# Attention, routed experts and dense experts in one kernel: the place of the norms, of the query tail, of the loads and of the first expert's number

## The chip, the cores and the metric

The kernel runs on one core of a Trainium2 chip. The metric is the device time of one execution in microseconds; before the change the median of three runs is 2073.45 us.

## The reference

Three parts follow each other, all in float32.

1. Attention over 4 batches of 8 heads, 576 tokens, head size 64: causal softmax attention, and a memory part `phi(q) @ M_prev / (phi(q) . z_prev + 1e-6)` with `phi(x) = max(x, 0) + min(exp(x), 1)`. The two are mixed by `g = sigmoid(beta)` of each head.
2. The 2304 rows of 512 go through a routed layer: `logits = x @ w_gate + modality_bias`, each row goes to the one of 8 experts with the highest logit, `relu(x @ w1) @ w2` with 1024 hidden columns, times the softmax weight of that expert.
3. A dense layer: all 8 experts see all rows, and their outputs are summed with weights from 8 rounds of row and column normalisation.

## The kernel before, in words

**Attention** (lines 27 to 490) works in 16 units `u`; one unit is two heads of one batch. Its instructions stand in an order written out by hand (`tc.manual_schedule()`), and each engine runs its own in that order. A unit is pipelined over two turns of the loop `for u in range(1, NU)`: in turn `u` the scores, maxima and exponentials of unit `u` are made, while unit `e = u - 1` is transposed, multiplied with its values and written, and keys and queries of `u + 1` are transposed.

The steps that matter here: `high(u)` and `low(u)` (scores of the four full query tiles, L226, and their masks, L333 and L342), `last_scores(u)` (the last 64 queries of both heads, L235), `top(u, i)` (row maxima on VectorE, L243 and L245), `exps(u, i)` (ScalarE, L257 and L259), `ptrans(e, k)` (TensorE transposes the probabilities, VectorE or ScalarE copies them out, L281, L289, L295, L296, L300), `tails` (the 64-row tails of keys, queries and phi(q), copies L210, L213, L214, L215), `memory(e, part)` (L309) and `av(e, part)` (L321, output L323). `phi_a` multiplies phi(q) by `z_prev` (VectorE L133, GpSimd L134), `phi_b` makes the norms from the sums of that product (VectorE L148 to L151) and scales the tail (GpSimd L153), `phi_c` brings in the softmax sums and scales the rest. `gate_v` (L141) scales the values, `relu` (L121) and `phi_e` (L126) prepare phi. `bank()` hands out four PSUM banks in turn (`ps_t`, 4 buffers), so a step may wait for the last reader of the bank four allocations back.

Part 0 of `memory` and `av` covers queries 0 to 255, part 1 the others (`SPAN`). `busy(n)` issues `n` matmuls of zeros, whose result nobody reads.

**Loads.** `load(u, names, eng)` issues three transfers for each of k, q and v: one for each head and one for the 64-row tails of both. `prepare()` issues unit 0's on the sync engine's queue (SP) and unit 1's on ScalarE's.

**Router.** `batch(g)` takes a group of 128-token tiles (`GROUPS`) once their attention is done: logits, softmax weight, one-hot of the expert, row numbers; each scaled tile is then scattered to its expert's region (GpSimd, L504). It is a generator, and the loop's `some()` runs one step. The last group runs behind the attention. `table()` then works out from the counts which tiles of which expert follow each other, and `rt.busy(64)` stands behind it.

**Routed experts** (`routed_experts`): `e0 = reg(0, 0, 0, ...)` reads the first expert's number from the table on SP, then SP issues two pieces of its `w1` (L856), the first tile's rows (L864, behind all scatters), and the other weights. TensorE transposes the rows (L878) and starts with L907. **Dense experts** follow.

Of the kernel before, what the change touches and what calls it, by code (L numbers as in the profile page):

```python
# [12 lines left out]
I32 = mybir.dt.int32  # L13
# [13 lines left out]
def attention(ctx, tc, q, k, v, M_prev, z_prev, beta, xT, ident, router):  # L27
# [10 lines left out]
    ps_t = es.enter_context(tc.tile_pool(name="ps_t", bufs=4, space=PSUM))  # L38


    qTp, Mb, Rs, vt = [], [], [], []
    nrm = [c1.tile([128, NT, 2], F32, name=f"nrm{i}") for i in range(2)]
    zeros = c1.tile([128, 512], BF16, name="zeros")
# [12 lines left out]
    def prepare():  # L56

        nc.vector.memset(zeros, 0.0)
        busy(12)
        gb = c1.tile([128, H], F32, name="gb")  # L60
        nc.scalar.dma_start(gb, beta[None, :].to_broadcast([128, H]))
        nc.gpsimd.memset(mk, 0.0)
        nc.gpsimd.affine_select(out=mk, in_=mk, compare_op=ALU.is_ge, fill=-1e9, base=0,
                                pattern=[[-1, 128]], channel_multiplier=1)
        for i in range(2):
            t = c1.tile([128, 640], F32, name=f"qTp{i}")
            nc.gpsimd.memset(t[:, 512:], 0.0)
            qTp.append(t)
        load(0, "kq")
        load(1, "kq", nc.scalar)  # L70
        nc.vector.tensor_copy(idb, ident)
        nc.vector.tensor_copy(mk2[0:64], mk[0:64, 0:64])
        nc.vector.tensor_copy(mk2[64:128], mk[64:128, 64:128])
        nc.scalar.activation(gt, gb, AF.Exp, scale=-1.0)
        nc.vector.tensor_scalar(gt, gt, 1.0, None, ALU.add)
        nc.vector.reciprocal(gt, gt)
        nc.vector.tensor_scalar(om, gt, -1.0, 1.0, ALU.mult, ALU.add)
        for i in range(2):
            t = c1.tile([128, NP, 128], F32, name=f"Mb{i}")
            nc.gpsimd.memset(t, 0.0)  # L80
            Mb.append(t)
        for i in range(3):
            t = c1.tile([128, NT, 128], F32, name=f"vt{i}")
            nc.gpsimd.memset(t[0:64, 4], 0.0)
            vt.append(t)
        for i in range(2):
            t = c1.tile([128, S], F32, name=f"R{i}")
            nc.gpsimd.memset(t[:, 512:], 1.0)
            Rs.append(t)
# [90 lines left out]
    def keys(u):  # L180

        p = bank("tp")
        turn(p, ld[u, "k"])
        un[u] = {"kT": tr.tile([128, S], F32, tag="kT", name="kT"), "P": {}}
        nc.vector.tensor_copy(un[u]["kT"][:, :512], p)
# [16 lines left out]
    def tails(u, un1):  # L202


        p = bank("tl")
        if u is not None:
            nc.tensor.transpose(p[:, 0:128], ld[u, "q"][:, 4], ident)
        if un1 is not None:
            nc.tensor.transpose(p[:, 128:256], ph[un1][1][:, 4], ident)
            nc.vector.tensor_copy(un[un1]["pT"][:, 512:], p[:, 192:256])  # L210
        if u is not None:
            qt = qTp[u % 2]
            nc.vector.tensor_copy(un[u]["kT"][:, 512:], p[:, 0:64])  # L213
            nc.scalar.activation(qt[0:64, 512:576], p[0:64, 64:128], AF.Copy, scale=0.125)  # L214
            nc.vector.tensor_scalar(qt[64:128, 576:640], p[64:128, 64:128], 0.125, None, ALU.mult)  # L215

    sc = {}

# [80 lines left out]
            nc.tensor.transpose(p[:, 0:128], PM[:, 448:576], ident)  # L299
            nc.vector.tensor_copy(un[u]["pt4"], p[:, 0:128].rearrange("p (h q) -> p h q", h=2))  # L300

    SPAN = ((0, 256), (256, S))

    def memory(u, part):

        b, a = divmod(u, NP)
        q0, q1 = SPAN[part]
        un[u]["x", part] = x = bank("x")
        nc.tensor.matmul(x[:, :q1 - q0], Mb[b % 2][:, a], un[u]["pT"][:, q0:q1], start=True, stop=False)  # L309

    def av(u, part):

        b, a = divmod(u, NP)
        pt, vn, x = un[u]["pt"], vt[u % 3], un[u]["x", part]
        q0, q1 = SPAN[part]
        nj = (2, 5)[part]
        for j in range(nj):
            for h in range(2):
                qs = max(q0, j * 128)
                rhs = pt[:, h, j, qs:q1] if j < 4 else un[u]["pt4"][:, h]  # L320
                nc.tensor.matmul(x[h * 64:(h + 1) * 64, qs - q0:q1 - q0], vn[:, j, h * 64:(h + 1) * 64], rhs,  # L321
                                 start=False, stop=(j == nj - 1))
        nc.vector.tensor_tensor(xT[:, a, b * S + q0:b * S + q1], x[:, :q1 - q0], Rs[u % 2][:, q0:q1], ALU.mult)  # L323
# [18 lines left out]
            nc.tensor.matmul(s[:, h, 128:384].rearrange("p (i k) -> p i k", i=2), idb,  # L342
                             mk[:, None, :].to_broadcast([128, 2, 128]), start=False, stop=True)

    NU = B * NP
    with tc.manual_schedule():
        prepare()
        keys(0)
        queries(0)
        tails(0, None)  # L350
        load_b(0)
        load(0, "v")
        rt = router()
        rt.ps, rt.busy = ps_t, busy
        relu(0)
        rt.constants()
        phi_e(0)
        load(1, "v")
        load(2, "kq")
        high(0)  # L360
        for i in (3, 2):
            top(0, i)
            exps(0, i)
        keys(1)
        queries(1)
        tails(1, None)
        busy(8)
        low(0)
        for i in (1, 0):
            top(0, i)  # L370
        phi_a(0)
        relu(1)
        gate_v(0)
        for i in (1, 0):
            exps(0, i)
        busy(3)
        last_scores(0)
        busy(8)
        phi_e(1)
        top(0, 4)  # L380
        phi_b(0)
        phi_c(0)
        phi_a(1)
        back = rt.biases()

        def some():
            next(back, None)

        def finish(u):
            exps(u, 4)  # L390
            norm(u)

        for u in range(1, NU):
            e, nx = u - 1, u + 1 < NU
            if nx:
                load(u + 1, "v")
            if u + 2 < NU:
                if (u + 2) % NP == 0:
                    load_b((u + 2) // NP)
                load(u + 2, "kq")  # L400
            if u < 3:
                rt.clear(u - 1)
            finish(e)
            gate_v(u)
            if nx:
                relu(u + 1)
            high(u)
            top(u, 3)
            some()
            ptrans(e, 5)  # L410
            ptrans(e, 4)
            exps(u, 3)
            ptrans(e, 0)
            top(u, 2)
            exps(u, 2)
            ptrans(e, 1)
            if nx:
                keys(u + 1)
                queries(u + 1)
            inverse(e)  # L420
            low(u)
            ptrans(e, 2)
            phis(e)
            top(u, 1)
            top(u, 0)
            ptrans(e, 3)
            some()
            phi_b(u)
            ptrans(e, 6)
            ptrans(e, 7)  # L430
            exps(u, 1)
            exps(u, 0)
            tails(u + 1 if nx else None, e)
            last_scores(u)
            if nx:
                phi_e(u + 1)
            top(u, 4)
            phi_c(u)
            some()
            if nx:  # L440
                phi_a(u + 1)
            else:
                finish(u)
            memory(e, 0)
            memory(e, 1)
            av(e, 0)
            av(e, 1)
            if u % NP == 0:
                for _ in back:
                    pass  # L450
                back = rt.batch(u // NP - 1, ps_t)
            del un[e]

        e = NU - 1
        for _ in back:
            pass
        ptrans(e, 0)
        ptrans(e, 1)
        inverse(e)
        ptrans(e, 2)  # L460
        phis(e)
        ptrans(e, 3)
        memory(e, 0)
        av(e, 0)
        ptrans(e, 5)
        ptrans(e, 4)
        back = rt.batch(3, ps_t)
        next(back)
        ptrans(e, 6)
        ptrans(e, 7)  # L470
        next(back)
        tails(None, e)
        memory(e, 1)
        next(back)
        av(e, 1)
        for _ in back:
            pass
        for _ in rt.batch(4, ps_t, True):
            pass
# [3 lines left out]
NE = 8  # L483
# [8 lines left out]
HT = 384  # L492
NG = N // (2 * HT)
GTL = 2 * HT // 128
GROUPS = [range(0, 4), range(4, 9), range(9, 13), range(13, 15), range(15, 18)]
WHY = "the table is worked out on the chip and stays within its bounds"
ET = mybir.EngineType

# [27 lines left out]
class Router:  # L526
# [21 lines left out]
    def constants(self):  # L548
# [21 lines left out]
        self.pos = c.tile([128, NTILE], I32, name="pos")  # L570
        self.tab = [c.tile([128, 4], I32, name=f"tab{i}") for i in range(2)]
        self.num = c.tile([1, 2], I32, name="num")

        self.table_parts()

# [133 lines left out]
    def table(self, ps):  # L709
# [15 lines left out]
                                th[:, None, :].to_broadcast([128, NE, M1]), ALU.is_gt)  # L725
        nc.vector.tensor_copy(cnt, tp)
        nc.vector.tensor_reduce(nt[:, :NE], gm, AX.X, ALU.add)
        left, big = t1([NE], "left"), t1([NE], "bigr")
        nc.vector.scalar_tensor_tensor(left, nt[:, :NE], -float(TB), cnt, ALU.mult, ALU.add)
        nc.vector.tensor_scalar(big, left, float(HB), None, ALU.is_gt)  # L730
# [63 lines left out]
def tile_attention_moe_moe(ctx, tc, q, k, v, M_prev, z_prev, beta, modality_id, w_gate1, modality_bias, w1a, w2a,  # L794
# [10 lines left out]
    with ExitStack() as actx:  # L805
# [2 lines left out]
        rt = attention(actx, tc, q, k, v, M_prev, z_prev, beta, xT, ident,  # L808
                       lambda: Router(actx, tc, c, xT, ident, modality_id, w_gate1, modality_bias))
        rt.table(rt.ps)  # L810
        rt.busy(64)

    big = ctx.enter_context(tc.tile_pool(name="big", bufs=1))
    X = big.tile([128, KD, XW], F32, name="X")
# [16 lines left out]
def routed_experts(ctx, tc, rt, ident, X, raw1, raw2, split, w1, w2, early):  # L831
# [184 lines left out]
            else:  # L1016
                nc.scalar.copy(yl, p.rearrange("p (h t) -> p h t", h=2))

    e0 = reg(0, 0, 0, (ET.SP,), NE - 1)
    for j in range(2):  # L1020
        load1(e0, j)
    xr, loads = load_x(0, 0)
# [425 lines left out]
```

## Time and profile before

| | |
|---|---|
| median of 3 runs | 2073.45 us (2072.9 to 2074.33) |
| the profiled execution | 2072.47 us |
| its span, first to last instruction | 2070.7 us |
| TensorE busy | 2017.4 us (97%) |
| VectorE, ScalarE, GpSimd busy | 1471.6, 850.8, 783.9 us |

Attention takes the first 275 us, the routed experts run to about 545 us, the dense ones to the end. An engine that is busy is not yet the one that bounds a stage; what shows that is which waits end last there. Each wait in the trace names the engine, its line, and the instruction that released it.

### The profile page before, as it was taken

What the parts mean: (1) busy time and instruction counts of PE and PEld (TensorE: products, weight loads), DVE (VectorE), ACT (ScalarE), POOL (GpSimd) and SP (SyncE); (2) the same over time, 40 slices, a digit from 0 to 9 for tenths busy, and PEclk for the clock granted to TensorE, in tenths of its full rate; (3) what the DMA queues carried; (4) which work ended last, traced back from release to release, by engine and by line L of the source; (5) the groups of instructions that cost most, each with busy time, mean ns of one, the idle gap of its engine ahead of it and who ended that gap; (6) DMA issues with size and microseconds to landing.
All of it is one profiled execution on the core that took longest, in us unless ns stands there. A gap on an engine that the chain in (4) does not pass through costs nothing.

```text
span 2070.7 us, 31467 instructions
## 1 busy us (share of the span) xinstructions
PE 2017.4 (97%) x11499; PEld 1773.3 (86%) x11499; DVE 1471.6 (71%) x2551; ACT 850.8 (41%) x1793; POOL 783.9 (38%) x761
## 2 busy tenths in 40 slices
PE   8998999998899999999999999999999999999998
PEld 5666669998699889988889988998898988998887
DVE  6877767665687776667796667777688676677775
ACT  4566545554634333333343333333343433333332
POOL 6666510000133344344464334334356333333332
PEclk9999999999999999999999999999999999999999
DMA  6333166556512233444432222222223122222221
GB/s 157 91 81 85 44 207 226 184 194 208 162 51 62 72 71 62 62 68 76 62 110 64 62 78 66 62 77 67 62 72 102 62 71 72 62 68 76 62 63 40
DMA packets 236157, 187.36 MB, mean 90 GB/s; under 512 B 69028, under 2 KB 191956, under 8 KB 235988
## 3 DMA queue, kind: packets, MB, share of 16 engines
q1 hardware_dynamic: 228772, 175.08, 30.6%
q0 software_dynamic: 3616, 9.49, 1.3%
q8 instruction: 95, 1.56, 0.3%
q10 hardware_dynamic: 3600, 0.63, 0.2%
q14 instruction: 74, 0.61, 0.1%
HBM read 171.51 MB, written 13.64 MB: 89 GB/s over the span
## 4 chain that ended last, share of the span: by engine, by line
issue 31%; PE 24%; POOL 17%; DMA 0%; DVE 0%; ACT 0%; POOLq 0%; SPq 0%; DVEq 0%
PE y L1250 13%; PE prod L1179 11%; POOL T L1071 8%; POOL w1l L1065 7%; POOL out_dram L504 1%; DMA r<-in_moe_w_dram 0%; PE lq L1291 0%; POOLq L1071 0%; POOL S L1149 0%; POOL S L1150 0%; POOL S L1151 0%; DVE w2l L1065 0%; POOL S4l L1065 0%; POOL S L1148 0%; PE lg L1303 0%
## 5 line engine op out<-in xcount | busy, mean ns | idle before, releaser
L1065 POOL TENSOR_TENSOR w1l<-T,w1h 128x1024 fp32r<-128x1024 f32 x94 | 226.7, 2411 | 842.5 <-ACT w1h L1065 842.5
L1197 ACT ACTIVATE hh<-c 128x384 fp32r<-128x384 f32 x384 | 202.1, 526 | 829.5 <-DVE c L1193 828.6
L1250 PE MATMUL y<-w2h,hh 128*128 128x512 f32 x1152 | 453.3, 394 | 0.0
L1250 PE MATMUL y<-w2l,hh 128*128 128x512 f32 x1152 | 453.3, 393 | 0.0
L1250 PE MATMUL y<-w2h,hl 128*128 128x512 f32 x1152 | 452.6, 393 | 0.0
L1202 DVE SCALAR_TENSOR_TENSOR hl<-c,hh 128x384 fp32r<-128x384 f32 x384 | 418.1, 1106 | 1.1 <-ACT hh L1197 0.8
L1193 DVE TENSOR_TENSOR c<-prod,u 128x384 f32<-128x384 f32 x288 | 160.0, 556 | 156.0 <-PE prod L1179 153.0
L1250 PEld LDWEIGHTS y<-w2h,hh 128*128 128x128 f32 x1152 | 216.2, 188 | 32.8
L1250 PEld LDWEIGHTS y<-w2h,hl 128*128 128x128 f32 x1152 | 216.3, 188 | 28.5
L1250 PEld LDWEIGHTS y<-w2l,hh 128*128 128x128 f32 x1152 | 216.4, 188 | 27.9
L1071 POOL TENSOR_TENSOR T<-r 128x256 f32<-128x256 f32 x188 | 161.6, 859 | 7.1
L1071 POOL TENSOR_TENSOR T<-r,T 128x256 f32<-128x256 f32 x188 | 158.7, 844 | 14.0 <-issue 6.9
L1193 DVE TENSOR_TENSOR u<-prod,u 128x384 f32<-128x384 f32 x192 | 105.7, 551 | 58.1 <-PE prod L1179 57.8
L1193 DVE TENSOR_TENSOR u<-prod,p 128x384 f32<-128x384 f32 x96 | 53.4, 557 | 129.6 <-PE prod L1179 128.3
L1065 DVE TENSOR_TENSOR w2l<-r,w2h 128x512 fp32r<-128x512 f32 x188 | 136.9, 728 | 0.6 <-ACT w2h L1065 0.6
L1065 ACT CAST w2h<-r 128x512 fp32r<-128x512 f32 x188 | 106.7, 609 | 0.0
L1193 DVE TENSOR_TENSOR c<-prod,p 128x384 f32<-128x384 f32 x96 | 53.5, 557 | 70.8 <-PE prod L1179 65.0
L1065 DVE TENSOR_TENSOR w1l<-r,w1h 128x512 fp32r<-128x512 f32 (+1 forms) x188 | 103.7, 551 | 0.0
L1065 ACT CAST w1h<-T 128x1024 fp32r<-128x1024 f32 x94 | 97.0, 1032 | 1.0 <-POOL T L1071 1.0
L1207 ACT COPY p<-prod 128x384 f32<-128x384 f32 x96 | 46.2, 481 | 123.4 <-PE prod L1179 122.1
L1261 DVE SCALAR_TENSOR_TENSOR acc<-y,P,acc 128x512 f32<-128x512 f32 x126 | 92.4, 743 | 4.3 <-PE y L1250 4.3
L1065 ACT CAST w1h<-r 128x512 fp32r<-128x512 f32 (+1 forms) x188 | 94.5, 503 | 0.0
(388 smaller groups left out, 4167.7 us busy)
## 6 DMA issues: line engine op xcount, KB each, us to landing
r<-in_moe_w_dram SPq DMA_DIRECT2D x188, 512.0 KB, 4.3
r<-in_moe_w_dram SPq DMA_DIRECT2D x188, 256.0 KB, 3.1
xr<-xs_sorted SPq DMA_DIRECT2D x22, 256.0 KB, 5.0
vt<-in_v_dram SPq DMA_DIRECT2D x32, 128.0 KB, 2.6
xs_sorted<-zrow SPq DMA_DIRECT2D x16, 256.0 KB, 3.1
kn<-in_k_dram SPq DMA_DIRECT2D x30, 128.0 KB, 2.7
qn<-in_q_dram SPq DMA_DIRECT2D x30, 128.0 KB, 3.2
zb<-in_z_prev_dram SPq DMA_DIRECT2D x4, 256.0 KB, 3.8
```

The source lines that it names most:

```text
L504: i = tc.nc.gpsimd.indirect_dma_start(out=out, out_offset=bass.IndirectOffsetOnAxis(ap=idx, axis=0), in_=src, in_offset=None)
L1065: return (lambda: nc.scalar.copy(hi, src)), (lambda: eng.tensor_tensor(lo, src, hi.bitcast(F32), ALU.subtract))
L1071: sub = lambda i, a, b: (lambda: nc.gpsimd.tensor_tensor(T[:, i], a, b, ALU.subtract))
L1179: nc.tensor.matmul(p, a[:, kd], b[:, kd], start=(i == 0), stop=(i == 5))
L1193: nc.vector.tensor_tensor(st[o], a, st[b], ALU.add)
L1197: nc.scalar.activation(hh[:, f, a * HT:(a + 1) * HT], st[o], AF.Relu)
L1202: nc.vector.scalar_tensor_tensor(hl[:, f, w], st[o], 0.0, hh[:, f, w].bitcast(F32), ALU.max, ALU.subtract)
L1207: nc.scalar.copy(st["p1"], p)
L1250: nc.tensor.matmul(yt[t], a[:, f, t * 128:(t + 1) * 128], b[:, f], start=(j == 0 and f == 0 and i == 0), stop=(j == NJ - 1 and f == 1 and ...
L1261: nc.vector.scalar_tensor_tensor(acc[t], yt[t], P[:, m, e:e + 1], acc[t], ALU.mult, ALU.add)
```

## The change

- Unit 0's queries load on ScalarE's queue and unit 1's keys on SP's; unit 1's queries load on ScalarE's queue behind the gate's exponential.
- The second half of the query tail is copied and scaled by ScalarE instead of VectorE.
- For the last unit alone, part 0 covers 320 queries; `ptrans(e, 4)` comes before `memory(e, 0)` there. The fourth router group takes three tiles, the last one two.
- `phi_a(0)`, `relu(1)` and `gate_v(0)` come before unit 1's keys.
- In the loop, `phi_b(u)` comes behind `top(u, 4)`, ahead of `phi_c(u)`.
- `table()` works out a new `head`, the first expert with a full tile, from the counts, and `e0` is read from that.
- `busy` is called with 6, 6 and 44 instead of 8, 8 and 64.

```diff
+    NU = B * NP
...
-        load(0, "kq")
-        load(1, "kq", nc.scalar)
+        load(0, "k")
+        load(0, "q", nc.scalar)
+        load(1, "k")
...
         nc.scalar.activation(gt, gb, AF.Exp, scale=-1.0)
+        load(1, "q", nc.scalar)
...
             nc.scalar.activation(qt[0:64, 512:576], p[0:64, 64:128], AF.Copy, scale=0.125)
-            nc.vector.tensor_scalar(qt[64:128, 576:640], p[64:128, 64:128], 0.125, None, ALU.mult)
+            nc.scalar.activation(qt[64:128, 576:640], p[64:128, 64:128], AF.Copy, scale=0.125)
...
-    SPAN = ((0, 256), (256, S))
+    def span(u, part):
+        cut = 256 if u + 1 < NU else 320
+        return ((0, cut), (cut, S))[part]
...
-        q0, q1 = SPAN[part]
-        nj = (2, 5)[part]
+        q0, q1 = span(u, part)
+        nj = -(-q1 // 128)
...
             exps(0, i)
+        phi_a(0)
+        relu(1)
+        gate_v(0)
         keys(1)
         queries(1)
         tails(1, None)
-        busy(8)
+        busy(6)
         low(0)
         for i in (1, 0):
             top(0, i)
-        phi_a(0)
-        relu(1)
-        gate_v(0)
         for i in (1, 0):
             exps(0, i)
         busy(3)
         last_scores(0)
-        busy(8)
+        busy(6)
...
             some()
-            phi_b(u)
             ptrans(e, 6)
             ptrans(e, 7)
...
             top(u, 4)
+            phi_b(u)
             phi_c(u)
...
         ptrans(e, 3)
+        ptrans(e, 4)
         memory(e, 0)
         av(e, 0)
         ptrans(e, 5)
-        ptrans(e, 4)
         back = rt.batch(3, ps_t)
...
-GROUPS = [range(0, 4), range(4, 9), range(9, 13), range(13, 15), range(15, 18)]
+GROUPS = [range(0, 4), range(4, 9), range(9, 13), range(13, 16), range(16, 18)]
...
+        self.head = c.tile([128, 1], I32, name="head")
...
         nc.vector.tensor_reduce(nt[:, :NE], gm, AX.X, ALU.add)
+        few, most = t1([NE], "few"), t1([1], "most")
+        nc.vector.scalar_tensor_tensor(few, nt[:, :NE], 0.0, self.e8, ALU.is_gt, ALU.mult)
+        nc.vector.tensor_reduce(most, few, AX.X, ALU.max)
+        nc.vector.tensor_scalar(self.head, most, -1.0, float(NE), ALU.mult, ALU.add)
...
-        rt.busy(64)
+        rt.busy(44)
...
-    e0 = reg(0, 0, 0, (ET.SP,), NE - 1)
+    e0 = nc.values_load(rt.head[0:1, 0:1], engines=(ET.SP,), min_val=0, max_val=NE - 1,
+                        skip_runtime_bounds_check_because=WHY)
```

## Rows read from the trace of the kernel before

**Rows 1.** The page's first line.
```profile
span 2070.7 us, 31467 instructions
```

**Rows 2.** Busy time of each engine by stretch (instructions), the loop; then clock, DMA share.
```profile
24.00:254.00 230.00, 208.63 (x1601) 148.40 (x1599) 178.11 (x462) 135.38 (x408) 144.43 (x134) 0.99 0.33 88
```

**Rows 3.** TensorE's waits, 24 to 254 us: who for whom, us in total, times, longest.
```profile
PE x L309 <- DVE pT L210: 8.9, 11, 1.4
PE x L309 <- DVE qTp L215: 3.3, 3, 1.1
PE xp L654 <- DVE pt L300: 3.2, 3, 1.3
PE rp__473 L172 <- DVE pt L281: 2.1, 1, 2.1
```

**Rows 4.** The same view for VectorE and ScalarE, one row of each.
```profile
DVE qTp L215 <- ACT qTp L214: 23.7, 14, 1.7
...
ACT pt L296 <- DVE pt L295: 32.8, 15, 3.1
```

**Rows 5.** Timeline, one turn without routing: start us, us, instruction, idle before and releaser.
```profile
75.72 0.81 DVE L148 TENSOR_REDUCE nrm<-ex 128x10 f32<-128x640 f32 x1
...
77.11 0.42 DVE L295 COPY pt<-tp 128x256 f32<-128x256 f32 x1
...
77.64 0.21 DVE L210 COPY pT<-tl 128x64 f32<-128x64 f32 x1
...
77.91 0.81 PE L309 MATMUL x<-pT,Mb 128*128 128x320 f32 x2 [0.59 <-DVE pT L210]
...
79.67 0.23 DVE L215 TENSOR_SCALAR qTp<-tl 64x64 f32<-64x64 f32 x1 [1.69 <-ACT qTp L214]
```

**Rows 6.** Timeline, a turn with routed tokens.
```profile
173.60 0.66 PE L654 MATMUL xp<-ident,xT 128*128 128x128 f32 x4 [1.31 <-DVE pt L300]
```

**Rows 7.** Timeline of the start.
```profile
1.30 1.16 ACTq L112 DMA_DIRECT2D kn<-in_k_dram  x2
...
2.64 1.87 SPq L112 DMA_DIRECT2D qn<-in_q_dram  x2
...
8.82 0.66 PE L172 MATMUL tp<-ident,qn 128*128 128x128 f32 x4 [2.97 <-DMA qn<-in_q_dram]
...
10.41 2.91 PE L226 MATMUL s<-kT,qTp 64*128 64x512 f32 x8
...
22.45 0.82 DVE L148 TENSOR_REDUCE nrm<-ex 128x10 f32<-128x640 f32 x1 [1.05 <-POOL ex L134]
```

**Rows 8.** Timeline of TensorE behind the attention.
```profile
271.90 1.47 PE L654 MATMUL xp<-ident,xT 128*128 128x128 f32 x12
...
274.92 13.97 PE L54 MATMUL busy<-zeros 128*128 128x512 bf16 x64
288.73 1.04 PE L878 MATMUL xtp<-ident,xr 128*128 128x128 f32 x8
```

**Rows 9.** SP behind the attention: table reads by line, timeline, landing of L864's transfers.
```profile
L851 SPq TENSOR_LOAD <-tab x3: 263/287/736, 279.1 to 281.4; - x3
...
280.02 1.02 SPq L856 DMA_DIRECT2D r<-in_moe_w_dram  x2
282.18 0.88 SPq L864 DMA_DIRECT2D xr<-xs_sorted  x2
...
DMA to landing us min/median/max: 3.9/3.9/4.0
```

**Rows 10.** TensorE at 240, 244 and 255 us, and the stretch at 240 by engine, its granted clock.
```profile
239.95 4.42 PE L321 MATMUL x<-pt,vt 128*64 128x256 f32 x28
244.30 1.77 PE L226 MATMUL s<-kT,qTp 64*128 64x512 f32 x8
...
254.92 2.92 PE L321 MATMUL x<-pt,vt 128*64 128x256 f32 x28
...
239.61:243.02 3.41, 3.41 (x17) 1.81 (x18) 1.66 (x6) 1.64 (x4) 2.61 (x4) 0.50 0.00 0
```

More of the change, by code (lines that the diff above doesn't have):

```diff
@@ L314, in av @@
         pt, vn, x = un[u]["pt"], vt[u % 3], un[u]["x", part]
-        q0, q1 = SPAN[part]
-        nj = (2, 5)[part]
+        q0, q1 = span(u, part)
+        nj = -(-q1 // 128)
         for j in range(nj):
@@ L343, in low @@
                              mk[:, None, :].to_broadcast([128, 2, 128]), start=False, stop=True)
-    NU = B * NP
     with tc.manual_schedule():
```

## The prediction

> **What bounds the kernel now.** Read first the page's head [rows 1]: one core, 2070.7 us from the first to the last instruction, the profiled execution itself 2072.47 us. The table by stage comes next: in the attention loop, 24 to 254 us, PE is busy 208.63 of 230 us, DVE 178.11 [rows 2]. So PE sets the pace there, and what counts is each stretch in which PE stands still. Behind the attention stage every start hangs on the one before it (the routed experts on the last tokens, the dense ones on the routed ones), so a microsecond won before the first routed matmul arrives at the end of the kernel, and nothing behind it is edited.
>
> The view of waits, limited to PE and the loop, shows what stops it [rows 3]: 11 times the matmul of `memory(e, 1)` (L309) waits for the DVE copy of the tail of the transposed queries (L210), 8.9 us in all; three times it waits for the copy L215 (3.3 us), and three times a transpose of routed tokens waits for L300 (3.2 us). All three releasers are DVE instructions that stand behind the norms in DVE's order. The reader is to see in [rows 5] why: `phi_b`, the norms, begins at 75.72, and the copies L295 and L210, whose inputs PE has by then, can only start at 77.11 and 77.64; PE gets its L309 at 77.91 after 0.59 us idle. The view of DVE's and ACT's own waits shows two more [rows 4]: DVE stands 1.7 us in 14 units before L215 because ACT's L214 comes first (23.7 us in all), and ACT stands 32.8 us before L296 because DVE's L295 comes first. Those alone cost nothing: PE isn't behind them, except through the bank that L215 frees.
>
> **The loop.** `phi_b` goes from before the copies to behind `top(u, 4)`. In [rows 5] it holds DVE from 75.72 to 77.11, so L295, L300, L210 and the key tail each come 1.39 us earlier. PE's largest wait for L210 is 1.4 us, in the first unit, and the mean of the 11 is 0.81, below 1.39; I take all 8.9 us. ACT's L296 follows L295, hence the exponentials of parts 1 and 0, the query tail and the next `exps(u, 4)` also come up to 1.39 us earlier. The query tail's second half moves from DVE (0.23 us) to ACT behind L214: one more small instruction on ACT, whose successor there is `phi_e`, then `exps(u, 4)`, both off PE's path; DVE loses the 1.69 us stall, and this is where the moved norms fit: 1.39 us into a hole of 1.69. In the three units that transpose routed tokens late, the wait for L300 is 1.31 us in [rows 6], and L309 then waits for the bank of the tails, whose last reader becomes ACT. That chain also comes 1.39 us earlier, but no more, so I take 3 x 1.4 = 4.2 of the 6.5 us. Sum 13.1 us. Who reads the norms: `phi_c` right behind them, then GpSimd's scaling of `qp`, which PE transposes in the next unit. GpSimd's first piece of it, `pv`, gets its norm later, and the copy of the reciprocals is queued behind that piece, but both moved with a stall that is gone. Ends: 6.5 us if the six waits of the last two rows stay and the 11 shrink by a quarter, 18 us if all 15.4 go and the heavy units' DVE backlog shrinks too.
>
> **The start.** Before, the sync queue issues the queries of unit 0 behind its keys, 2.64 to 4.51 us, while ACT issues the keys of unit 1 from 1.30 to 2.46; PE then waits 2.97 us for those queries [rows 7]. After, ACT issues the queries of unit 0 in that first place, and the keys of unit 1 go behind the keys of unit 0. By issue alone the two large pieces end 4.51 - 2.46 = 2.05 us earlier; with the other unit's packets now behind them it can be all 2.97. I take 2.6. [...] What it costs: ACT issues the three pieces of unit 1's queries behind the gate's exponential, before it can copy unit 0's queries, and PE's transposes of both units' queries stand behind that; it may take back up to 1 us, which the lower end covers.
>
> The eight score matmuls right behind that wait took 2.91 us [rows 7] against 1.77 us [rows 10] for the same eight at the full clock; PE had just stood for 2.97 us. With the wait gone I take the 1.1 us; ends 0 and 1.14. `phi_a(0)`, `relu(1)` and `gate_v(0)` go ahead of unit 1's keys on DVE and GpSimd. The product for unit 0's norms came so late that DVE waited 1.05 us for it at 22.45 [rows 7], and then a transpose of PE waited 2.1 us for DVE, the last of [rows 3]. GpSimd's later pieces for unit 0 all move up with it. I take 2.1, ends 0 and 2.1. The two pairs of zero matmuls are 4 x 13.97/64 = 0.9 us of PE [rows 8]; both bursts end in a wait for ACT's exponentials, so I cost them at 0.1, and the query tail on ACT at 0.4 for the maxima behind it. Sum 6.3 us; ends 2.1 and 8.
>
> **The tail.** PE runs 64 zero matmuls in 13.97 us, 218 ns each, and the first transpose of routed tokens follows at 288.73 with no wait [rows 8]: the zeros set it. The tokens had landed: issued from 282.18, the second 0.5 us later, 3.9 to 4.0 us each, so by 286.7 [rows 9]. With 44, PE is free 20 x 0.218 = 4.4 us earlier, at 284.4 plus what the steps before them shift. Regrouping: the cut at 320 makes tokens up to tile 15 complete in the first part, so the fourth group has three tiles and the last one two. The last group's transposes fall from 1.47 us [rows 8] by a third, and its scatters from three to two; but group four's extra four transposes now stand ahead of it in PE's order, and `memory(e, 0)` waits less because the moved transposes of `ptrans(e, 4)` fill PE there. I cost this at +0.3 us for the start of the zeros, ends -0.6 and +0.8.
>
> The tokens must then land earlier too. Sync's chain: it reads the expert's number from 279.1, issues two weight pieces from 280.02, reads two more table entries, and issues the tokens at 282.18 [rows 9]. The new `head` needs only the counts; the counts' matmuls end where the zeros begin, 274.92, and with their copy and reduction and three small DVE instructions, none dearer than L215's 0.23 us, `head` stands at about 276.3, so the weights go out some 2.8 us earlier, and the tokens wait for the table itself, which these three push back by up to 0.7 us: issue at about 281.4. No weights compete by then; with 3 to 4 us to land, the second piece is there at 284.9 to 285.9. I take the first transpose at 285.1, 3.6 us earlier; ends 1.9 (landing as before) and 4.4.
>
> **Sum.** 13.1 + 6.3 + 3.6 = 23.0 us off 2072.47, 2049.5. The median of the three runs is 2073.45, 1.0 above the profiled one; so 2050.5.
>
> **Rivals.** First, DVE takes PE's place: it is busy 178.11 of the 230 us [rows 2], the routing's steps fall into some units alone, and the rp row of [rows 3] shows a transpose of PE that waits for DVE's backlog. If half of the loop's term is given back so, 2050.5 + 6.6 = 2057. Chance 0.14.
>
> Second, the clock. [...] Chance 0.08; the opposite, that the stretch at 239.61 goes, is worth 1.5 us and lies in my range.
>
> Third, slower: DVE's stall isn't removed but passes to `phi_c`, which needs the sums of the same exponentials. If ACT doesn't come earlier, because L296 waits for PE rather than for L295, the norms lie bare on DVE behind the last maximum, and the next unit's first maximum and all behind it come 1.39 us later, 15 times: 20.9 - 9.9 = 11 us slower, 2084.5. It decides once DVE's backlog behind the mask matmuls exceeds the 1.69 us it had. Against it: ACT's wait names L295 in 15 units [rows 4]. Chance 0.04.
>
> Fourth, the edit of the loop does nothing for PE, since another bank is late next and `memory(e, 1)` waits for ACT's part of the copies: 2050.5 + 13.1 = 2063.6. The 11 waits end on L210, not on L215 or ACT, against it. Chance 0.06.
>
> **How the numbers follow.** My forecast has 0.65, the four rivals 0.32, and 0.03 is left for a loss in the loop that cancels the rest. All ends together give 2073.45 - 30.4 = 2043 and, with the loop at 8.9 and the other two low, 2060.5; the range 2042 to 2063 takes in the first two rivals. A measurement of this kernel tells about 0.2%, 4 us, from no change: faster 0.93, same 0.03, slower 0.04.
>
> **What would show it.** Right: in the loop's waits the rows for L309 and L300 fall under 3 us together, L215 is gone from DVE, and a unit like that of [rows 5] is 0.6 us shorter; unit 0's queries are transposed before 6.5 us; the first routed transpose follows the zeros by under 1 us and no longer touches them. Wrong: `phi_b` followed by new waits of PE for xT or the exponentials; a first score as late as 10 us; a lower clock in the first routed expert.

## The result and the profile after

The kernel after takes **2044.33 us** (median of 4 runs, 2040.58 to 2045.09), the kernel before 2073.18 (2072.7 to 2074.33): ratio 0.9856, 95% interval 0.9839 to 0.9874. That is 28.85 us less, where 23.0 were forecast; the predicted 2050.5 is 6.2 us too high and the range held the time. The two profiled executions differ by 28.4 us in their spans. Cut at starts that both traces show (the reduction of a unit's last maximum, L245 and L248 after; the zeros; the first matmul of a product), this is where it lies:

| stretch | before, us | after, us | difference |
|---|---|---|---|
| start to the last maximum of unit 1 | 38.04 | 30.90 | -7.1 |
| from there to the last maximum of unit 15 (the loop) | 216.0 | 199.2 | -16.8 |
| from there to the zeros | 20.9 | 21.1 | +0.2 |
| zeros to the first routed matmul | 15.1 | 13.8 | -1.3 |
| from there to the first matmul of the small tiles | 222.1 | 219.2 | -2.9 |
| from there to the last instruction | 1558.6 | 1558.0 | -0.5 |

The first row holds 1.4 us that the prediction counts under the loop: the first unit's wait for L210, the longest of [rows 3], which is gone.

The head of the page of the kernel after, against [rows 1]:

```profile
span 2042.3 us, 31433 instructions
...
PE 2007.1 (98%) x11478; PEld 1771.3 (87%) x11478; DVE 1471.2 (72%) x2539; ACT 855.9 (42%) x1809; POOL 782.9 (38%) x761
```

**The loop.** The rows by source line give the first and last of the 15 maxima; before, then after:

```profile
L245 DVE TENSOR_REDUCE nm<-s x15: 747/758/758, 38.0 to 254.0; 128x1 f32<-128x576 f32 x15
```

```profile
L248 DVE TENSOR_REDUCE nm<-s x15: 750/758/759, 30.9 to 230.1; 128x1 f32<-128x576 f32 x15
```

PE's waits of the kernel after in the loop, 24 to 231 us (total, times, longest), against [rows 3]. The releasers L210 and L300 are gone (they would be L213 and L303 now); of the 15.4 us in three rows, 2.5 are left:

```profile
PE x L314 <- ACT qTp L218: 2.5, 3, 1.1
PE s L229 <- ACT P L260: 1.4, 4, 0.8
PE rp__470 L175 <- DVE pt L284: 1.0, 1, 1.0
PE rp__1404 L175 <- DVE pt L284: 0.2, 1, 0.2
```

DVE's and ACT's waits after, 21 to 238 us, against [rows 4]. DVE no longer waits for ACT's half of the query tail, and ACT's wait for L298 (L295 before) has shrunk to a third of its 32.8 us:

```profile
DVE nm L246 <- PE s L338: 12.0, 11, 1.2
ACT pt L299 <- DVE pt L298: 10.5, 12, 1.2
```

The timeline of the light unit after (start, duration), against [rows 5]. The order is now L298, L213, then the maximum L248, and the norms (L151) only at 70.72, when PE has already had its L314 for 0.9 us. PE runs straight into it from the scores, and the unit takes 13.02 us from maximum to maximum instead of 13.87:

```profile
68.85 1.14 PE L238 MATMUL s<-kT,qTp 128*128 128x288 f32 x4
68.94 0.42 DVE L298 COPY pt<-tp 128x256 f32<-128x256 f32 x1
...
69.47 0.22 DVE L213 COPY pT<-tl 128x64 f32<-128x64 f32 x1
69.85 1.22 PE L314 MATMUL x<-pT,Mb 128*128 128x256 f32 x4
...
70.72 0.81 DVE L151 TENSOR_REDUCE nrm<-ex 128x10 f32<-128x640 f32 x1
```

**The start.** The timeline of PE and ACT's queue after, 0 to 20 us, against [rows 7]: unit 0's queries are issued from 1.30, the first scores run at 7.59 instead of 10.41, and in 1.77 us. But six zero matmuls at 12.54 take 2.69 us:

```profile
1.30 1.16 ACTq L115 DMA_DIRECT2D qn<-in_q_dram  x2
...
7.59 1.77 PE L229 MATMUL s<-kT,qTp 64*128 64x512 f32 x8 [0.36 <-ACT qTp L195]
...
11.96 0.63 PE L175 MATMUL tp<-ident,qn 128*128 128x128 f32 x4 [1.82 <-DMA qn<-in_q_dram]
12.54 2.69 PE L55 MATMUL busy<-zeros 128*128 128x512 bf16 x6
```

Up to the small tiles, the table by stretch after (busy time of PE, weight loads, DVE, ACT, GpSimd with counts, granted clock, DMA share, GB/s) has two stretches at clock 0.50, one in the start and one in the first routed expert. Each follows on a wait of PE for a transfer (1.82 and 2.29 us). The stretch at 239.61 before [rows 10] has gone:

```profile
12.62:16.02 3.40, 3.40 (x11) 1.41 (x11) 0.98 (x3) 2.28 (x9) 3.40 (x3) 0.50 0.67 147
265.20:268.61 3.41, 3.41 (x16) 3.26 (x16) 2.53 (x5) 1.74 (x4) 0.00 (x0) 0.50 1.04 378
```

**The tail.** PE's timeline after, against [rows 8]: the zeros take 9.66 us, but the first transpose of routed tokens now stands 2.29 us for their landing, where before it followed the zeros with no wait:

```profile
251.18 9.66 PE L55 MATMUL busy<-zeros 128*128 128x512 bf16 x44
...
263.13 0.33 PE L887 MATMUL xtp<-ident,xr 128*128 128x128 f32 x1 [2.29 <-DMA xr<-xs_sorted]
...
264.99 1.28 PE L916 MATMUL h1p<-xh,w1l 128*128 128x256 f32 x4 [0.24 <-ACT xh L826]
```

The sync queue's timeline after, against [rows 9]: the weights go out at 2.1 us behind the zeros' start instead of 5.1, the tokens at 9.2 instead of 7.3.

```profile
253.29 0.98 SPq L865 DMA_DIRECT2D r<-in_moe_w_dram  x2
260.36 0.88 SPq L873 DMA_DIRECT2D xr<-xs_sorted  x2
```

Its waits there say why: the issue of the tokens stood for the last scatter.

```profile
SPq L873 <- DMA xs_sorted<-xr,row: 2.9, 1, 2.9
```

**A place nobody edited.** At the branch into the small tiles, PE's waits before (490 to 530 us) and after (470 to 510 us); "issue" is time in which PE waited for nothing that the profile shows, PEq is its sequencer:

```profile
PE h1r L985 <- issue: 6.2, 1, 6.2
```

```profile
PE h1r L994 <- PEq L1055: 1.9, 1, 1.9
PE h1r L994 <- issue: 1.4, 1, 1.4
```

### The profile page after: what moved, and what is told of

It reads as the page before. It is cut to its first block, busy times and chain, and to the rows that moved or that the text cites. A ratio compares the mean times of both kernels' runs of the same rounds, so it can differ in the third digit from the quotient of the medians.

```text
span 2042.3 us, 31433 instructions
## 1 busy us (share of the span) xinstructions
PE 2007.1 (98%) x11478; PEld 1771.3 (87%) x11478; DVE 1471.2 (72%) x2539; ACT 855.9 (42%) x1809; POOL 782.9 (38%) x761
## 3 DMA queue, kind: packets, MB, share of 16 engines
q8 instruction: 95, 1.56, 0.3%
## 4 chain that ended last, share of the span: by engine, by line
issue 32%; PE 25%; POOL 17%; DVE 0%; ACT 0%; POOLq 0%; DVEq 0%
PE y L1260 13%; PE prod L1189 11%; POOL T L1081 8%; POOL w1l L1075 7%; POOL out_dram L508 1%; PE lq L1301 0%; POOLq L1081 0%; POOL S L1159 0%; POOL S L1161 0%; POOL S L1160 0%; DVE w2l L1075 0%; POOL S4l L1075 0%; POOL S L1158 0%; PE lg L1313 0%; DVE S2l L1075 0%
## 5 line engine op out<-in xcount | busy, mean ns | idle before, releaser
L1260 PEld LDWEIGHTS y<-w2h,hh 128*128 128x128 f32 x1152 | 216.2, 188 | 32.8
```

The costliest lines, as they stand in the source:

```text
L1260: nc.tensor.matmul(yt[t], a[:, f, t * 128:(t + 1) * 128], b[:, f], start=(j == 0 and f == 0 and i == 0), stop=(j == NJ - 1 and f == 1 and ...
```

## The experiments

The theory: the loop's gain is the norms put into a hole that the query tail's move makes, so each alone gives much less; in the tail, the early weights go ahead of the last scatter and hold back the tokens. The rivals: the query tail alone carries the loop; the scatter is late for another reason; and the zeros' 20 x 0.218 us come out somewhere, either at the first routed matmul or not at all. Single totals of this kernel spread too far to tell 2 us (the kernel after ran between 2040.6 and 2046.4 in all its runs), so what follows rests on stretches of the traces, taken between starts as in the table above. There is one trace of each kernel, and two of the change. How far such a stretch can be trusted differs: the loop took 199.2 to 199.4 us in all eleven traces that leave it as changed, while zeros to first routed matmul took 13.1 to 14.0 us in the seven traces that leave that part as changed.

**1. The norms back ahead of the copies**, the rest as after:

```diff
             some()
+            phi_b(u)
             ptrans(e, 6)
...
             top(u, 4)
-            phi_b(u)
             phi_c(u)
```

> The changed kernel with phi_b back ahead of the copies L298 to L303; all else as changed. Theory (the place of the norms in VectorE's order is what TensorE waited for): the stretch from unit 1's to unit 15's last maximum, 199.2 us in the changed kernel against 216.0 before, grows by 11 to 16 us; TensorE's waits of memory(e, 1) for VectorE come back; the whole run is 11 to 16 us slower than the changed kernel. Rival (the query tail on ScalarE alone brings it, through VectorE's stall): the stretch grows by under 5 us.

The loop took 214.7 us, the run 2059.13. PE's waits, 24 to 246 us, show the old releaser under its new number, and L303 (L300 before) with it:

```profile
PE x L314 <- DVE pT L213: 8.5, 12, 1.0
PE xp L659 <- DVE pt L303: 3.2, 3, 1.3
PE x L314 <- ACT qTp L218: 3.2, 3, 1.1
```

So the query tail on ACT alone is worth 216.0 - 214.7 = 1.3 us, and the place of the norms 15.5 on top of it. A part of the 15.5 is a stretch at the lower clock, which this kernel has as well (granted clock 0.57 from 168 to 172 us) and the change has not.

**2. The query tail's half back on DVE**, the norms in their new place:

```diff
-            nc.scalar.activation(qt[64:128, 576:640], p[64:128, 64:128], AF.Copy, scale=0.125)
+            nc.vector.tensor_scalar(qt[64:128, 576:640], p[64:128, 64:128], 0.125, None, ALU.mult)
```

> The changed kernel with the second half of the query tail on VectorE again. Theory (the moved norms fit because VectorE's stall of 1.69 us is gone): the stall comes back in about 14 units, and since the norms now stand behind it, TensorE gets its output late in the units where VectorE has a backlog: the stretch from unit 1's to unit 15's last maximum grows by 3 to 10 us. Rival A (the norms' place alone does it): it grows by under 2 us. Rival B (my third rival of the prediction, the norms lie bare in every unit): by over 15 us.

The loop took 206.4 us, the run 2051.17: 7.1 us of the gain go. The stall of [rows 4] is back on DVE (waits, 24 to 238 us), and PE now waits for a copy behind it, three times:

```profile
DVE qTp L218 <- ACT qTp L217: 23.6, 14, 1.7
```

```profile
PE tp L283 <- DVE xT L328: 4.5, 3, 1.5
PE x L314 <- DVE qTp L218: 2.6, 3, 1.1
```

The norms alone are worth 9.7 us, the tail alone 1.3, both 16.8: together they give 5.8 us more than the two alone. This looks like the mechanism of the slower rival, in small: with the stall kept, PE gets new waits for DVE's copies. That it is the moved norms which push them there was not traced.

**3. The expert's number from the table again**, with 44 zeros:

```diff
-    e0 = nc.values_load(rt.head[0:1, 0:1], engines=(ET.SP,), min_val=0, max_val=NE - 1,
...
+    e0 = reg(0, 0, 0, (ET.SP,), NE - 1)
```

> The changed kernel with the first expert's number read from the finished table, so the weights are issued about 3 us later. Theory (the early weights stand ahead of the last scatter's packets in the DMA engines, so the sync queue waited 2.88 us for the scatter): that wait is gone, the tokens are issued about 1 to 2 us earlier, counted from the start of the zeros (9.18 us in the changed kernel), and the first routed matmul comes 0 to 2 us earlier than its 13.8 us behind the start of the zeros. Rival (the early weights help as I had predicted): the first routed matmul comes 2 to 3 us later.

The run took 2040.86 us. The sync queue issued weights and tokens 2.1 us apart, and the tokens were there when the zeros ended. The zeros took 11.0 us here instead of 9.66: the lower clock fell into them (0.50 and 0.72 in their first two stretches of 2 us), and none followed in the first expert. Sync's timeline, then PE's:

```profile
254.47 0.98 SPq L865 DMA_DIRECT2D r<-in_moe_w_dram  x2
256.59 0.88 SPq L873 DMA_DIRECT2D xr<-xs_sorted  x2
```

```profile
262.19 0.99 PE L916 MATMUL h1p<-xh,w1l 128*128 128x256 f32 x4 [0.24 <-ACT xh L826]
```

The first routed matmul stands 12.6 us behind the start of the zeros, against 13.8 after. The early number costs about 1.2 us there (0.5 against the lowest of the seven traces) instead of winning any. From the zeros to the end of the trace this kernel is 1.6 and 0.9 us shorter than the two traces of the change, too little to call it faster from one run.

**4. Four orders of weights and tokens**, with the early number: the tokens ahead of all weights (tokens_first); one piece of weights, then the tokens (one_early); the same with the tokens' transposes and copies ahead of the split of the second piece (one_early_x); and the change itself, taken again beside it.

```diff
-    for j in range(2):
-        load1(e0, j)
+    load1(e0, 0)                  # one_early; tokens_first: behind the tokens
     xr, loads = load_x(0, 0)
...
+    load1(e0, 1)
...
-        if j == 1:                # one_early_x: at the first piece
             for kp in range(2):
```

> The changed kernel with the tokens' two transfers issued ahead of all weights of the first expert; the early number is kept. Theory (the weights delayed the last scatter): the tokens are issued 5.5 to 7 us behind the start of the zeros instead of 9.18, the first transpose follows the zeros with a gap under 1 us, and the first routed matmul, which now needs the weights that come behind, is at 11.5 to 13.5 us instead of 13.8. Rival (the scatter was late for another reason): the tokens are issued as late as before, and the first routed matmul comes 2 us later or more.

> The changed kernel with one weight piece of 512 KB issued ahead of the tokens instead of two, the second behind them. Counted from the start of the zeros, the tokens go out at 9.18 us in the changed kernel, at 6.09 with no weights ahead. Theory (the packets of the weights run ahead of the last scatter, about 1.4 us per piece): the tokens go out at 6.5 to 8, the first transpose follows the zeros at 9.6 to 11, and the first routed matmul is at 11.5 to 12.5, earlier than with two pieces ahead (13.80), with none (15.21) and with the late number (12.64). Rival (any early weight piece holds the scatter to the end): tokens at 9, matmul at 13.5 or later.

> One weight piece ahead of the tokens, and the tokens' transposes ahead of the second piece's split in ScalarE's and VectorE's order (with one piece ahead alone, the split of the second held the tokens' split, and the first routed matmul fell to 15.41 us behind the zeros' start). Theory: first transpose at 10 to 11 us, first routed matmul at 11.6 to 12.6 us instead of 13.80; the whole run 1 to 2.5 us faster than the changed kernel of the same call. Rival (the second piece, which now comes later, is late for the third group of matmuls): the first matmul comes early, but the hundredth is no earlier than the 40.3 us of the changed kernel.

> The changed kernel itself, for times of the same call and a second trace. Expected by every theory: a median of 2041 to 2046 us, and a first routed matmul 13 to 14.5 us behind the zeros' start; whether the clock falls in the first 20 us may differ from the first trace, with unit 1's last maximum at 29.2 us without and 30.9 with it.

In us behind the start of the zeros:

| kernel | weights issued | tokens issued | first routed matmul | 100th |
|---|---|---|---|---|
| before (64 zeros) | 5.1 | 7.3 | 15.1 | 40.2 |
| after | 2.1 | 9.2 | 13.8 | 40.3 |
| the same, again | 2.1 | 9.3 | 13.8 | 40.0 |
| number from the table | 4.9 | 7.0 | 12.6 | 38.1 |
| tokens first | 7.2 | 6.1 | 15.2 | 42.3 |
| one piece first | 2.1 | 7.7 | 15.4 | 42.5 |
| one piece first, transposes early | 2.1 | 7.5 | 12.0 | 39.9 |

The hundredth is that of the first layer (L907, L916 after). The fewer pieces go out ahead of the tokens, the earlier these are issued: at 6.1 us with none, 7.5 and 7.7 with one, 8.5 to 9.5 in the eight traces with two early pieces and the change's groups. That is what the theory says of the last scatter. What was expected of the first matmul was missed twice. With the tokens first (11.5 to 13.5 expected, 15.2 found) the weights became late: ACT's copy of the tokens stood behind their split, and PE waited 4.7 us for it. With one piece first (11.5 to 12.5 expected, 15.4 found) that copy stood behind the split of the second piece, and PE waited 3.4 us for it. Taking that out brought the earliest first matmul of all. But then PE waited for the split of its own results (L920), which DVE makes behind the split of the weights, and as the rival had it, the hundredth was hardly earlier than in the change (timeline of PE):

```profile
261.33 0.99 PE L916 MATMUL h1p<-xh,w1l 128*128 128x256 f32 x4 [0.24 <-ACT xh L826]
...
267.31 0.74 PE L916 MATMUL h1p<-xh,w1l 128*128 128x256 f32 x4 [0.69 <-DVE hl L920]
```

Over four runs each: one_early_x 2042.64 us (2042.37 to 2044.16, 4 runs), ratio 0.9853 (0.9837 to 0.987); the change 2043.91 (2042.03 to 2046.39, 4 runs), ratio 0.9861 (0.9845 to 0.9878). The two can't be told apart. Tokens first ran in 2045.88, one piece first in 2045.95.

**5. All 64 zeros again:** `rt.busy(64)`.

> The changed kernel with 64 zero matmuls behind the router's table. Theory for the start of the experts: the first transpose waits for the zeros, 13.9 us behind their start instead of 11.95, the first routed matmul at 15.1 instead of 13.80, and the clock doesn't fall there. Theory for the branch into the small tiles (the place of TensorE's instructions decides how its code is fetched there): its wait is as long as before, the first h1r matmul 221.5 to 223 us behind the first h1p, against 222.10 before and 219.24 in the changed kernel. Rival (that difference is chance or the clock): 218 to 220 us again.

The first routed matmul came 15.1 us behind the start of the zeros and the run took 2048.46. At the 100th routed matmul the kernel with 44 zeros had won nothing over this one (40.0 or 40.3 against 40.2 us). The difference opens at the branch into the small tiles, whose first matmul stood 222.2 us behind the first routed one, inside the 221.5 to 223 expected; PE's waits, 470 to 520 us:

```profile
PE h1r L994 <- issue: 6.3, 1, 6.3
```

**6. 44 zeros and 20 more of 8 columns**, half a microsecond of work:

```diff
-    def busy(n):
+    def busy(n, w=512):
...
         rt.busy(44)
+        rt.busy(20, 8)
```

> The changed kernel with 20 more zero matmuls of 8 columns behind the 44, which take about 0.5 us but put the later instructions of TensorE as far back as 64 do. Theory (the place of the instructions decides the wait at the branch into the small tiles): that wait is 6 us again, and the first h1r matmul is 221 to 223 us behind the first h1p, against 219.24. Rival (what 64 zeros change is time or clock, not place): 218 to 220 us.

The wait was back although the zeros' end and the first routed matmul (14.0 us behind their start) were those of the change; the run took 2049.35. The first matmul of the small tiles came 224.6 us behind the first routed one, later than the 221 to 223 expected: 1.3 us more than after were lost on the first hundred routed matmuls, and 4.0 at the branch. PE's waits, 470 to 520 us:

```profile
PE h1r L995 <- issue: 5.9, 1, 5.9
```

PE stands idle there for 5.9 to 6.3 us in the three kernels with 64 matmuls behind the table (before, and these two), and for 1.8 to 2.3 us in all eleven others, whose branch comes at 480 to 499 us, ahead of these two and behind them. From the hundredth routed matmul to the last instruction the three take 1755.6 to 1756.5 us and the eleven 1750.2 to 1751.8. Behind the long wait the small tiles began at the lower clock in all three (0.50 to 0.52 over 4 us). Behind the short one the clock differed: 1.00 in both traces of the change and with the old loads, 0.57 to 0.69 in the other eight. The stretches of 4 us from the first of their matmuls, in this kernel and after:

```profile
488.20:492.20 4.00, 3.94 (x18) 3.97 (x19) 0.08 (x1) 1.00 (x3) 0.00 (x0) 0.51 0.92 287
```

```profile
484.20:488.20 4.00, 2.56 (x20) 2.50 (x21) 3.78 (x6) 3.11 (x7) 0.00 (x0) 1.00 0.72 240
```

**7. The start in parts:** the old order of loads (loads_back), and `phi_a(0)`, `relu(1)`, `gate_v(0)` behind the first maxima again (phia_back).

```diff
-        load(0, "k")                          # loads_back
-        load(0, "q", nc.scalar)
-        load(1, "k")
+        load(0, "kq")
+        load(1, "kq", nc.scalar)
...
-        load(1, "q", nc.scalar)
...
-        phi_a(0); relu(1); gate_v(0)          # phia_back: moved behind
+        phi_a(0); relu(1); gate_v(0)          # top(0, 1) and top(0, 0)
```

> The changed kernel with the loads of units 0 and 1 on their former queues. Theory (the queries of unit 0 are late because of their place): the first score matmul, at 7.59 us in the changed kernel, moves to 10 to 10.7, and unit 1's last maximum, at 30.90, moves 1.5 to 3.5 us later. Rival (the rest of the start absorbs it): unit 1's last maximum moves by under 0.7 us.

> The changed kernel with phi_a(0), relu(1) and gate_v(0) back behind the first maxima. Theory (their place made VectorE wait for GpSimd and TensorE for VectorE): unit 1's last maximum comes 1 to 3 us later than its 29.2 us (30.9 where the clock falls in the first 20 us), and a transpose of unit 0 waits for VectorE again. Rival (the earlier loads alone bring it): under 0.5 us later.

Without the new loads the first score matmul stood at 9.75 us (10 to 10.7 expected; before 10.41), against 7.59 and 7.96 in the two traces of the change and 7.15 to 8.16 in all twelve with the new loads. The last maximum of unit 1 stood at 31.4, against 30.9 and 29.3. The granted clock fell in this trace too, from 10.1 to 13.5 us (0.62 over 9.5 to 14), as it did at 12.6 in the trace with 30.9; the one with 29.3 has no such stretch. So the loads are worth 1.6 to 3.3 us at the first score. At unit 1's last maximum it is 0.5 us between the two traces that have the lower clock, which is what the rival said, and 2.1 against the one without it: whether the loads are worth more than the 0.5 there depends on whether their order brings the lower clock, and that stays open. The old place of `phi_a` brought the 2.1 us wait of the rp row of [rows 3] back, and the maximum came at 30.4, 1.1 us later than in the trace of the change that has no stretch at the lower clock; this one has none either (its six zeros took 1.46 us at 12.56). The runs took 2045.08 and 2044.69.

**8. The groups as before:** the cut at 256 queries, groups (13, 15) and (15, 18), `ptrans(e, 4)` behind `ptrans(e, 5)`.

```diff
-        cut = 256 if u + 1 < NU else 320
+        cut = 256
...
-GROUPS = [range(0, 4), range(4, 9), range(9, 13), range(13, 16), range(16, 18)]
+GROUPS = [range(0, 4), range(4, 9), range(9, 13), range(13, 15), range(15, 18)]
```

> The changed kernel with the last unit parted at 256 queries again, two tiles in the fourth router group and three in the last, and the transposes of ptrans(e, 4) behind ptrans(e, 5). Theory (what the shorter last group saves, the longer fourth takes from TensorE): from unit 15's last maximum to the first zero matmul it is 20.6 to 21.2 us, as in both kernels (21.05 and 20.88); but the last scatter goes out 1.3 us later, at 3.8 to 4.0 us behind the first zero instead of 2.60, so the tokens go out 0.5 to 1.5 us later than the 9.18 of the changed kernel. Rival (the regrouping is worth a microsecond that something else hid): that stretch is 22 us or more.

The zeros began 20.95 us behind unit 15's last maximum, against 21.05: no difference. With three scatters in the last group the tokens are issued later still (9.8 against 9.2 us), and the first routed matmul came 14.7 us behind the zeros' start, against 13.8. The run took 2043.74.

## Why the prediction was right in sum and wrong in two of its terms

**The loop, 13.1 forecast, 16.8 found.** The mechanism was right: the norms in a hole that the tail's move opens, and every wait on L210 and L300 in the loop gone. The table by stretch shows what the sum lacked. From unit 1's last maximum to unit 15's, PE was busy 198.20 of 216.01 us before and 194.45 of 199.23 after:

```profile
38.04:254.05 216.01, 198.20 (x1523) 140.51 (x1519) 166.39 (x436) 127.79 (x384) 133.36 (x123) 0.99 0.32 83
```

```profile
30.90:230.13 199.23, 194.45 (x1536) 141.97 (x1536) 166.58 (x422) 135.13 (x410) 133.27 (x123) 1.00 0.36 92
```

Its idle time fell by 13.0 us, which is what was forecast. In part this is luck: the forecast's 13.1 holds the first unit's 1.4 us, which lie ahead of this stretch, and it lacks the 0.9 us by which three waits on the copy L281 shrank. The other 3.7 us are busy time, at which the sum put nothing. A part of it comes with each wait. Before, the last two matmuls of the memory part that PE runs ahead of the wait stand at 76.64, and the two behind it at 77.91, 0.81 us long [rows 5]:

```profile
76.64 0.68 PE L309 MATMUL x<-pT,Mb 128*128 128x256 f32 x2
```

From 76.64 to 77.91 + 0.81 = 78.72 are 2.08 us; the same four matmuls after take 1.22 in one piece. The wait cost 0.86, not its idle row of 0.59: 0.27 us of busy time go with it. In each of the five units without routed tokens PE's busy time fell by 0.26 or 0.27 us, 1.3 in all. The stretch at the lower clock at 239.61, 1.5 us by the 4.42 against 2.92 of [rows 10], lies in the loop too and is gone. The rest of the 3.7 us is in the units with routed tokens and was not parted.

**The start, 6.3 forecast, 7.1 and 8.8 found** (two traces of one kernel; 1.4 us of both belong to the loop's term). The upper end of 8 is more than its parts give: 2.97, 1.14 and 2.1 with the zeros and the query tail in full make 7.5. Queries were taken at 2.6; the traces give 1.6 to 3.3 at the first score, which can't tell the 2.05 us of issue alone from 2.6. `phi_a`'s order, 2.1, gave 1.1: half of the transpose's wait is left. The term of the clock was wrong as a step. The first scores did run at granted clock 1.00 (1.77 us), but in two of the twelve traces with the new loads (after, and tokens first) the lower clock (0.50 after) came 5 us later, at 12.6, and in the other ten not at all. Six zeros took 2.69 us there and 1.46 in the second trace of the change, and unit 1's last maximum differs by 1.6 us. Part of the spread of the runs lies here.

**The tail, 3.6 forecast at the first transpose and 3.9 for the part behind the zeros' start; 1.7 and 1.9 found, and 1.3 at the first routed matmul.** The start of the zeros is right (+0.2 against +0.3). What failed is "the tokens wait for the table itself, which these three push back by up to 0.7 us: issue at about 281.4. No weights compete by then". The tokens wait for the scatters too, and these the early weights overtook. The last scatter was issued at 253.78, 0.5 us behind the weights. The rows by source line, times from issue to landing (minimum, median, maximum) of scatters: before (278 to 280 us), after (253 to 255), and with the number from the table again (251 to 254):

```profile
DMA to landing us min/median/max: 2.8/2.9/3.0
```

```profile
DMA to landing us min/median/max: 3.3/4.8/6.3
```

```profile
DMA to landing us min/median/max: 3.0/3.0/3.1
```

Scatter 6.3 us, tokens issued at 260.36, PE empty for 2.29 us, and behind that granted clock 0.50 from 265.20 to 268.61, in the first expert. From the first to the hundredth routed matmul it took 26.42 us, against 24.95 before: this is the second rival, the clock, at about the 1.5 us that such a stretch costs in [rows 10]. By the 100th routed matmul nothing is left of the 3.6 us. That the early weights did it is shown by experiment 3, which moved them alone and had both the scatters' 3.0 us and the first matmul back, and by experiment 4, where the tokens' issue follows the number of early pieces.

**What wasn't forecast: the branch, about 4 us.** From the start of the prediction on I held that nothing behind the first routed matmul is edited, so that nothing there changes. But PE's program ahead of the branch became 21 matmuls shorter (24 zeros fewer; the cut at 320 adds 3), and its wait fell from 6.2 to 1.9 us, with 1.4 more a little later. Experiments 5 and 6 part length of program from time: 20 matmuls of almost no duration bring the 5.9 us back. The trace has a queue for instructions, with 95 packets in 1.56 MB, 16 KB each, and dates them. In the three kernels with the long wait one such packet starts 7.1 to 7.6 us ahead of the first matmul of the small tiles and the next 2.7 us ahead, when PE has been idle for over 3 us. In the eleven with the short wait they start 10.0 to 11.7 and 3.1 to 3.6 us ahead, the second before PE goes idle. That the second of these brings what stands behind the branch, and is asked for only once PE is idle in the three, is then my likely reading, but no run shows it: the trace doesn't say which instructions a packet holds. So leaving out the 20 zeros behind the table was worth about what was forecast for it (20 x 0.218 = 4.4), at another place and for another reason, and this is luck: from the zeros' start to the last instruction it is 1796.6 us with 64 of them in experiment 5, and 1791.1 and 1790.4 in the two traces of the change.

**The other rivals.** DVE did not take PE's place: 173.80 us busy from 24 to 231, where PE was busy 201.09. The loop's edit was not idle, and the slower rival did not come: with the query tail undone 7.1 us of the gain went, and the loop was still 9.7 us faster than before. What would show it: the waits on L309 and L300 fell to 2.5 us, under the 3 named; L215's wait is gone; the unit of [rows 5] is 0.85 us shorter, where 0.6 was named; the queries are transposed at 6.52, not before 6.5; the first routed transpose follows the zeros by 2.29 us, not under 1; and the first expert has the lower clock (0.50), which was named as a sign of being wrong, and was one for the tail.

## What to carry to other kernels

Move work into a stall together with the edit that frees the stall: here the halves of the pair alone gave 1.3 and 9.7 us, both 16.8. Before issuing a transfer earlier, list what must land ahead of its neighbours in the same stretch; 1 MB of weights moved up by 3 us cost the last small scatter 3 us (6.3 us to land, against 3.1 in experiment 3), and the weights weren't needed yet. And after a change in the number of instructions of an engine, look at its next branch before explaining the total.

## What the runs showed of the hardware that I had not expected

- A branch of PE cost 1.8 to 2.3 us in eleven kernels and 5.9 to 6.3 in three, depending on some 20 matmuls of the program ahead of it. Behind the long wait the granted clock was 0.50 to 0.52 over the next 4 us; behind the short one it was between 0.57 and 1.00.
- Packets of the GpSimd queue hardly moved beside those of a large load on the hardware queues, for 2.6 us: 1 against 862, where the 1.5 us ahead moved 79 against 38 and the 2.3 us behind 80 against 156. The DMA rows after, 255.3 to 257.9 us (packets, MB, share of the engines), while the last scatter was under way:

```profile
q1 hardware_dynamic: 862, 0.87, 102.0%
...
q0 software_dynamic: 1, 0.00, 0.0%
```

Whether the scatter's packets were ready by then, or were only written late, was not tried and stays open.
